# Half of one streamed weight chunk made resident, paid for with the output tail's second buffer and P_pad's own, with the tail's heads and stores moved to suit

## The chip, the cores and the metric

The kernel runs on one core of a Trainium2 chip. Times are device microseconds; lower is better. Every ratio compares fast runs of a kernel with fast runs of the kernel before on the same chip, one after the other. The experiments ran in five rounds on five chips: e1 to e4; e6 to e9 with e8; e10 to e13; e14 to e19; f29 and f3. Where two changed kernels of different rounds are compared below (e6 with e1, e13 with e6, e14 with e10), it is their ratios that are compared, and single profiled runs give the stage times. Ratios are the mean time of one kernel's fast runs over the mean time of the other's fast runs of the same rounds, so they are not quite the ratio of the medians quoted beside them. Brackets give the 95% interval of a ratio.

## The reference, cut to what matters

Two independent computations are joined along the last axis. The first (a long convolution) fills about the first 460 us and is not touched by the change. The second is a recurrent transformer: 64 segments of 32 new rows plus 8 memory rows go through a 32-head attention, and 8 rows of each result are the memory of the next segment.

```python
for s in range(n_seg):                       # 64 segments, strictly one after the other
    h = jnp.concatenate([mem, xs], axis=1)   # 8 memory rows + 32 rows of x
    q, k, v = (einsum('btd,dhe->bhte', h, W) for W in (Wq, Wk, Wv))
    scores = where(mask, einsum('bhqe,bhke->bhqk', q, k) * scale, -1e9)
    o = einsum('bhqk,bhke->bhqe', softmax(scores), v)
    o = einsum('bhte,hed->btd', o, Wo)
    mem = o[:, :M, :]                        # what the next segment waits for
    outs.append(o[:, M:, :])
```

## The kernel before: the parts that matter

The weights of the recurrent part are cut into 64 chunks of 128 partitions x 2048 bf16 (512 KB). In the order of use: 8 K, 8 Q (first half of the heads), 8 K, 8 Q (second half), 16 V, 16 output projection chunks. 43 stay in on-chip memory. 21 are "streamed"; two of these are kept in spare PSUM, so 19 are loaded from HBM in every segment, through a ring of six slots. A slot is refilled when PE has used its chunk:

```python
STREAM = (0, 1, 3, 7, 11, 15, 21, 23, 25, 29, 33, 36, 40, 43, 46, 49, 51, 53, 59, 60, 62)
KEPT = {18: "A", 6: "B"}          # positions in STREAM: chunks 59 and 21 are kept in PSUM
TURN = (6, 4)
INLINE = {1: 0, 3: 1, 5: 0, 11: 1, 12: 0, 14: 1}
...
def done(ch):                     # after the last matmul that reads chunk ch
    if ch in streamed:
        ...
        free.append(live.pop((now[0], ch))[0])
        ...
        if nxt in kept and s > 0: unkeep(s, kept[nxt])    # copy back from PSUM into the free slot
        else: fetch()                                     # start the next load
```

In each segment PE computes 32 of the 40 rows directly. The other eight, the last rows of each segment, are set aside in OTB and projected for two segments at once: the "output tail", 32 heads of four matmuls, one tail for a pair of segments. I call the first segment of a pair even, the second odd. The tail of a pair was run during the next pair: `TURN[0]` heads ahead of the hand-over of memory to the next segment, `TURN[1]` behind it, and the heads whose chunk is streamed while that chunk is in its slot ("inline"), three chunks in each segment. Its result goes out over the last rows of segments whose 32 rows (`Y`) were stored before.

```python
def store(self):
    YB = one.tile([128, 256], BF, tag="QT", name="YB")
    nc.vector.tensor_copy(YB[:], self.acc)
    for dq in range(4):
        nc.gpsimd.dma_start(...rows SEG*NB*b + NX ... of both segments..., YB[32 * dq:32 * dq + W, :])
...
hT, KBs, QBs = pend.pop(s)
VBs = one.tile([128, 2, 128], BF, tag="VBs", name="VBs")          # the V record, at the top of a segment
nc.gpsimd.dma_start(VBs[:]..., VBD[s]...)
...
Y = one.tile([128, 256], BF, tag="PT", name="Y")
nc.scalar.copy(Y[:], yacc[:, 0:256])
...
    tail.run(TURN[0])
    fill_mem(pend[s + 1][0], Y)                                   # the hand-over: rec <- tps <- Y
nc.gpsimd.dma_start(..., Y[:])
    tail.run(TURN[1])
```

A tile with a tag takes the memory of the last tile with that tag, and its first write waits until everything that used the old one has finished, DMA included. The instructions of each engine are issued in the order in which the program has them.

## Time and profile before

The median was 2196.6 us. The loop's hand-overs run from 459.4 us to 2156.6 us on the profile's scale.

| 700 to 2150 us | before |
|---|---|
| DMA share of 16 engines, rate | 1.01, 389 GB/s |
| PE busy | 1170 of 1450 us (81%) |
| DVE, ACT busy | 36%, 26% |
| granted TensorE clock | 0.99 |
| mean segment, even and odd (segments 10 to 59) | 26.46 and 26.99 us |

Windows view of the kernel before, the loop between 700 and 2150 us. Columns: the stretch and its length, then busy us and number of instructions of each engine, granted clock, DMA share, GB/s.

```profile
core 0: us, PE busy (x) PEld busy (x) DVE busy (x) ACT busy (x) POOL busy (x), PEclk, DMA share, GB/s
700.00:2150.00 1450.00, 1170.47 (x28793) 669.07 (x28781) 528.60 (x1904) 373.44 (x706) 257.38 (x811) 0.99 1.01 389
```

PE is idle a fifth of the time. The waits of PE in the same stretch (us in total, times, longest) say that it waits for streamed loads more than for anything else:

```profile
PE acc L873 <- DMA wring<-WS: 97.5, 218, 1.8
PE yacc L959 <- DMA wring<-WS: 47.7, 88, 1.6
PE SB L819 <- DVE SB L798: 28.8, 28, 1.2
PE SB L819 <- DVE SB L810: 17.7, 25, 0.7
```

The third line is tail heads that wait for the score masks to be written into the same PSUM bank, the fourth tail heads that wait for the tail's sums in that bank to be set to zero. Issues of DMA, from the page: size, and median us from issue to landing.

```profile
wring<-WS SPq DMA_DIRECT2D x1216, 512.0 KB, 7.4
VBs<-VBD POOLq DMA_DIRECT2D x64, 64.0 KB, 6.3
out_dram<-Y POOLq DMA_DIRECT2D x64, 64.0 KB, 6.3
out_dram<-YB POOLq DMA_DIRECT2D x128, 8.0 KB, 5.0
```

Each of these, even the one of 8 KB, has a median of 5 us or more to landing.

### The profile page before, as it was taken

The numbers are of one execution on the slowest core, as the hardware profiler recorded it, in microseconds if no ns is written. First come the engines' busy times: TensorE is split into PE (matmuls) and PEld (weight loads), VectorE is DVE, ScalarE is ACT, GpSimd is POOL, SyncE is SP. The second block draws the span as 40 slices with busy tenths as digits, with TensorE's granted clock in tenths as the row PEclk, the third lists the DMA queues.
The fourth block names the chain that finished last, engine by engine and source line by source line (L and its number), as shares of the span: only waits on it lengthen the run. The fifth ranks groups of instructions, "written<-read, shape, count | busy, mean of one in ns | idle before, by whom it ended". The sixth has DMA issues, their size and how long they took to land. (4 is left out here: it accounts for less than half of the span.)

```text
span 2195.6 us, 81532 instructions
## 1 busy us (share of the span) xinstructions
PE 1739.5 (79%) x35636; PEld 930.1 (42%) x35636; DVE 874.0 (40%) x2686; ACT 648.3 (30%) x1139; POOL 444.4 (20%) x1139
## 2 busy tenths in 40 slices
PE   4687886878778878788888887887878787888886
PEld 2232233334444444444444444444544444444444
DVE  8836752123333333333333333333333333333333
ACT  7845530122222222222222222222222222222222
POOL 5013432201112111111111111111112211111111
PEclk9888998999999999999999999999999999999999
DMA  9998869979999999999999999999999999999997
GB/s 336 338 346 297 279 230 331 336 262 395 373 380 388 382 383 391 389 386 384 390 392 395 392 394 390 392 396 386 390 383 386 389 383 383 392 392 383 386 389 270
DMA packets 261678, 804.66 MB, mean 366 GB/s; under 512 B 52332, under 2 KB 52364, under 8 KB 261319
## 3 DMA queue, kind: packets, MB, share of 16 engines
q1 hardware_dynamic: 227816, 721.58, 86.2%
q0 software_dynamic: 28272, 67.31, 9.2%
q10 hardware_dynamic: 5232, 10.55, 1.5%
q8 instruction: 279, 4.57, 0.9%
q14 instruction: 79, 0.65, 0.1%
HBM read 739.92 MB, written 62.39 MB: 365 GB/s over the span
## 5 line engine op out<-in xcount | busy, mean ns | idle before, releaser
L873 PEld LDWEIGHTS <-rec 128*32 128x32 bf16 x12351 | 322.4, 96 | 470.9 <-issue 252.0
L873 PE MATMUL acc<-wring,rec 128*32 128x512 bf16 (+1 forms) x3777 | 375.6, 385 | 137.0 <-DMA wring<-WS 123.7
L882 ACT CAST qkv_sb<-acc 128x512 bf16<-128x512 f32 x384 | 225.1, 586 | 657.1 <-PE acc L873 657.1
L959 PEld LDWEIGHTS <-OT 128*32 128x32 bf16 x8192 | 218.7, 97 | 181.0 <-issue 153.2
L959 PE MATMUL yacc<-wring,OT 128*32 128x256 bf16 x3072 | 154.7, 277 | 100.7 <-DMA wring<-WS 58.5
L873 PE MATMUL acc<-Wmid,rec 128*32 128x512 bf16 x3072 | 226.6, 385 | 0.0
L873 PE MATMUL acc<-Wres,rec 128*32 128x512 bf16 x2816 | 222.3, 382 | 0.0
L819 PEld LDWEIGHTS <-OTB 128*16 128x16 bf16 x4096 | 104.9, 90 | 102.8 <-issue 92.6
L945 ACT CAST OT<-OTp 128x512 bf16<-128x512 f32 x128 | 75.1, 586 | 242.1 <-PE OTp L937 242.1
L975 DVE COPY KT<-tps 128x512 bf16<-128x512 bf16 x64 | 27.2, 425 | 298.7 <-PE tps L888 298.7
L774 POOL DMA_DIRECT2D rec<-REC x64 | 37.5, 585 | 519.4 <-issue 282.7
L946 DVE CAST OTB<-OTp 128x128 bf16<-128x128 f32 x128 | 37.4, 292 | 260.4 <-ACT OT L945 260.4
L725 DVE TENSOR_SCALAR wring<-OTp 128x384 int32<-128x384 int32 x126 | 112.3, 891 | 59.3 <-PE acc L873 49.0
L873 PE MATMUL acc<-pw,rec 128*32 128x512 bf16 x1536 | 130.3, 382 | 0.0
L849 POOL COPY KT<-rec 128x128 bf16<-128x128 bf16 x128 | 38.8, 303 | 426.8 <-PE SB L897 422.7
L834 POOL DMA_DIRECT2D out_dram<-YB x128 | 73.3, 579 | 238.5 <-DVE YB L832 225.3
L903 DVE TENSOR_REDUCE mx<-SB 128x5 f32<-128x200 f32 x128 | 47.1, 368 | 175.8 <-PE SB L897 175.8
L819 PE MATMUL SB<-wring,OTB 128*16 128x256 bf16 x1488 | 78.8, 275 | 39.7 <-DVE SB L798 32.6
L888 PE MATMUL tps<-ident,qkv_sb 128*128 128x128 bf16 x1024 | 101.0, 221 | 8.2 <-DVE wring L725 0.2
L888 PEld LDWEIGHTS <-qkv_sb 128*128 128x128 bf16 x1024 | 62.7, 97 | 105.6 <-ACT qkv_sb L882 65.4
L1015 ACT CAST Y<-yacc 128x256 bf16<-128x256 f32 x64 | 23.8, 373 | 248.0 <-PE yacc L959 244.1
L959 PE MATMUL yacc<-Wlate,OT 128*32 128x256 bf16 x2048 | 94.4, 276 | 2.2 <-issue 2.1
(231 smaller groups left out, 2706.3 us busy)
## 6 DMA issues: line engine op xcount, KB each, us to landing
wring<-WS SPq DMA_DIRECT2D x1216, 512.0 KB, 7.4
rec<-REC POOLq DMA_DIRECT2D x64, 192.0 KB, 6.1
SK<-s_sb SPq DMA_DIRECT2D x16, 512.0 KB, 5.9
SU<-s_sb SPq DMA_DIRECT2D x16, 512.0 KB, 4.9
Kg<-SK ACTq DMA_DIRECT2D x32, 256.0 KB, 4.8
Ug<-SU SPq DMA_DIRECT2D x32, 256.0 KB, 5.3
REC<-stage POOLq DMA_DIRECT2D x16, 512.0 KB, 9.0
SZ<-zs SPq DMA_DIRECT2D x31, 256.0 KB, 5.2
```

What stands on the lines that cost most here:

```text
L725: nc.vector.tensor_scalar(out=dst, in0=src, scalar1=0, scalar2=None, op0=ALU.bitwise_or)
L774: nc.gpsimd.dma_start(rec[:], REC[:, s, :])
L819: nc.tensor.matmul(self.acc[32 * dq:32 * dq + W, x - o:y - o], lhsT=self.OTB[:, c, 4 * g + i, :], rhs=r, start=first and not self.seeded, ...
L834: nc.gpsimd.dma_start(bass.AP(outb.tensor, outb.offset + (SEG * NB * self.b + NX) * 2048 + 256 * dq, [[2048 * SEG, NB], [2048, 8], [1, 256 ...
L849: nc.gpsimd.tensor_copy(KT[:, :, :, 32:40], KBs[:, 128 * g:128 * g + 128].rearrange("p (c i t) -> p i c t", c=4, i=4))
L873: nc.tensor.matmul(self.acc[32 * c:32 * c + 32, x - 512 * c:y - 512 * c], lhsT=hT[:, kc, :], rhs=r, start=(kc == 0 and x == 512 * c), stop ...
L882: nc.scalar.copy(sb[:], self.acc[:])
L888: nc.tensor.transpose(tp[:, i * 128:(i + 1) * 128], sb[:, i * 128:(i + 1) * 128], ident[:])
L903: nc.vector.tensor_reduce(out=mx[:], in_=S, op=ALU.max, axis=AX.X)
L945: nc.scalar.copy(OT[:], o_view[:, :, :, 0:32])
L946: nc.vector.tensor_copy(OTB[:, :, 4 * g:4 * g + 4, 8 * j:8 * j + 8], o_view[:, :, :, 32:40])
L959: nc.tensor.matmul(yacc[32 * dq:32 * dq + 32, x - o:y - o], lhsT=OT[:, c, i, :], rhs=r, start=(h == 0 and x == o), stop=(h == 31), tile_po ...
```

## The change

The intent is to stream less: half of chunk 3 (a K chunk) becomes resident, 256 KB fewer per segment. That needs 2 KB per partition. By the tile sizes, a single OTB frees 1 KB, and P_pad, which now shares the slots of QT and KT, 640 B; the pool of the softmax's two small tiles also goes from two buffers to one, and they share one tag. The tail's result, which had shared QT's slot, is now stored from the slot of the V record. With one OTB, the tail of a pair has to be finished before the next pair writes OTB, so its heads move up: all inline heads into the odd segment, 4 and 6 at the odd-to-even turn, 10 in the next K projection. Core of the diff:

```diff
-TURN = (6, 4)
-INLINE = {1: 0, 3: 1, 5: 0, 11: 1, 12: 0, 14: 1}
+TURN = (4, 6)
+HALF = 3
...
+    half = order[HALF]
+    WH = ring.tile([128, 1024], BF, name="WH")
+    nc.gpsimd.dma_start(WH[:], dram_chunk(half)[:, 0:1024])
...                                          # fetch(): columns 1024 to 2048 only, for that chunk
-    two = ctx.enter_context(tc.tile_pool(name="b_two", bufs=2, side="right", reuse_waits="tile"))
+    two = ctx.enter_context(tc.tile_pool(name="b_two", bufs=1, side="right", reuse_waits="tile"))
...
-    P_pad = one.tile([128, 5, 64], BF, name="P_pad")
-    nc.vector.memset(P_pad[:], 0.0)
...
-                YB = one.tile([128, 256], BF, tag="QT", name="YB")
+                YB = one.tile([128, 256], BF, tag="VBs", name="YB")
...
-            VBs = one.tile([128, 2, 128], BF, tag="VBs", name="VBs")     # top of the segment
-            nc.gpsimd.dma_start(VBs[:]..., VBD[s]...)
...
-            def softmax_a():
+            def softmax_a(g):
+                P_pad = one.tile([128, 5, 64], BF, tag="KT" if g else "QT", name="P_pad")
+                nc.gpsimd.memset(P_pad[:, 0:4, 32:64], 0.0)
...                                          # softmax_b: seed_scores() taken out
-                        if last or INLINE[hp] == j:
+                    if j == NB - 1 and ch in streamed:
                             tail.head(2 * hp, w)
...
-            k0 = Proj(0, 0).run().evac()
+            k0 = Proj(0, 0)
+            for n in (3, 3, 32, 0):
+                k0.run(2)
+                more_tail(n)                 # in even segments; the last head triggers store()
+            k0 = k0.evac()
             q0 = Proj(1, 0).run(4)
             KT0 = keys(0)
             last_queries(0)
+            VBs = one.tile([128, 2, 128], BF, tag="VBs", name="VBs")
+            nc.gpsimd.dma_start(VBs[:]..., VBD[s]...)
...
+            if j == NB - 1:
+                tail = Tail(OTB, b)          # its zeroing, now in the middle of the odd segment
...
+            PT0 = softmax_b(P0)
+            seed_scores()                    # masks for the second half of the heads
...
-            if j == NB - 1 and not last:
-                tail = Tail(OTB, b)
...
                 fill_mem(pend[s + 1][0], Y)
+                seed_scores()                # masks for the next segment
```

More of the change, by code (lines that the diff above doesn't have):

```diff
@@ L644, in fetch @@
             live[s, ch] = k, t = slot()
-            (nc.gpsimd if k > 3 and s == 0 and len(live) < 3 else nc.sync).dma_start(t[:], stream_src(ch))
+            c = slice(1024 if ch == half else 0, 2048)
+            eng = nc.gpsimd if k > 3 and s == 0 and len(live) < 3 else nc.sync
+            eng.dma_start(t[:, c], stream_src(ch)[:, c])
     def place(ch, ap):
@@ L742, in pieces @@
         t = live[now[0], ch][1]
+        if ch == half:
+            return [(0, 1024, WH[:]), (1024, 2048, t[:, 1024:2048])]
         if kept.get(ch) == "B" and now[0] > 0:
@@ L803, in b_kernel, with __init__ @@
         class Tail:
-            def __init__(self, OTB, b, acc=None):
-                self.OTB, self.b, self.acc = OTB, b, tacc if acc is None else acc
-                self.seeded = acc is None
+            def __init__(self, OTB, b):
+                self.OTB, self.b, self.acc = OTB, b, tacc
                 self.left = list(range(32))
@@ L813, in head @@
                 g, c, i = h // 16, (h % 16) // 4, h % 4
-                first = len(self.left) == 32
                 self.left.remove(h)
@@ L820, in head @@
                                          lhsT=self.OTB[:, c, 4 * g + i, :], rhs=r,
-                                         start=first and not self.seeded, stop=not self.left,
+                                         start=False, stop=not self.left,
                                          skip_group_check=True, tile_position=(0, 32 * dq))
@@ L836, in store @@
                                 [[2048 * SEG, NB], [2048, 8], [1, 256]]), YB[32 * dq:32 * dq + W, :])
-        OTB = tail = own = None
+        OTB = tail = None
         for s in range(n_seg):
@@ L843, in b_kernel @@
             hT, KBs, QBs = pend.pop(s)
-            VBs = one.tile([128, 2, 128], BF, tag="VBs", name="VBs")
-            nc.gpsimd.dma_start(VBs[:].rearrange("p g e -> p (g e)"), VBD[s].rearrange("t c i w -> (c i) t w"))
             def keys(g):
@@ L906, in softmax_a, with softmax_b @@
                 nc.scalar.activation(S, S, ACT.Exp, scale=scale)
-            def softmax_b():
-                ssum = two.tile([128, 5], F32, tag="ssum", name="ssum")
+                return P_pad
+            def softmax_b(P_pad):
+                ssum = two.tile([128, 5], F32, tag="mx", name="ssum")
                 nc.vector.tensor_reduce(out=ssum[:], in_=S, op=ALU.add, axis=AX.X)
@@ L925, in softmax_b @@
                     nc.vector.transpose(out=PT[:, kb, :, 32:40], in_=P_pad[:, 4, ks])
-                seed_scores()
                 return PT
@@ L961, in out_proj, with more_tail @@
                                                  tile_position=(0, 32 * dq))
-                    if tail is not None and 2 * hp in tail.left and (ch in streamed or last):
-                        if last or INLINE[hp] == j:
-                            tail.head(2 * hp, w)
-                            tail.head(2 * hp + 1, w)
-                    if own is not None and ch in streamed:
-                        own.head(2 * hp, w)
-                        own.head(2 * hp + 1, w)
-                    done(ch)
-            k0 = Proj(0, 0).run().evac()
+                    if j == NB - 1 and ch in streamed:
+                        tail.head(2 * hp, w)
+                        tail.head(2 * hp + 1, w)
+                    done(ch)
+            def more_tail(n):
+                if tail is not None and j == 0:
+                    tail.run(n)
+            k0 = Proj(0, 0)
[3 more added lines that the diff above has]
+            k0 = k0.evac()
             q0 = Proj(1, 0).run(4)
@@ L974, in b_kernel @@
             last_queries(0)
+            VBs = one.tile([128, 2, 128], BF, tag="VBs", name="VBs")
+            nc.gpsimd.dma_start(VBs[:].rearrange("p g e -> p (g e)"), VBD[s].rearrange("t c i w -> (c i) t w"))
             nc.vector.tensor_copy(KT0[:, :, :, 0:32], transposes(k0))
@@ L981, in b_kernel @@
             scores(0, QT0, KT0)
-            softmax_a()
+            P0 = softmax_a(0)
+            if j == NB - 1:
+                tail = Tail(OTB, b)
             q1 = Proj(1, 1).run(4)
@@ L986, in b_kernel @@
             nc.scalar.copy(KT1[:, :, :, 0:32], transposes(k1))
-            PT0 = softmax_b()
+            PT0 = softmax_b(P0)
+            seed_scores()
             q1 = q1.run(4).evac()
@@ L993, in b_kernel @@
             scores(1, QT1, KT1)
-            softmax_a()
+            P1 = softmax_a(1)
             pv1 = Proj(2, 1).run(4)
             if j == 0:
-                OTB_new = one.tile([128, 4, 8, 8 * NB], BF, tag=f"OTB{b % 2}", name="OTB")
-                OTB = OTB_new
+                OTB = one.tile([128, 4, 8, 8 * NB], BF, tag="OTB", name="OTB")
             attend(0, PT0, V0)
             OT0 = evac_o(0)
-            PT1 = softmax_b()
+            PT1 = softmax_b(P1)
             pv1.run(4)
@@ L1006, in b_kernel @@
             yacc = ps_acc.tile([128, 512], F32, tag="acc", name="yacc")
-            if last:
-                own = Tail(OTB, b, ps_acc.tile([128, 512], F32, tag="acc", name="own_acc")[:, 0:256])
             out_proj(range(0, 5), OT0)
@@ L1015, in b_kernel @@
             nc.scalar.copy(Y[:], yacc[:, 0:256])
-            if j == NB - 1 and not last:
-                tail = Tail(OTB, b)
-            if tail is not None and not last:
+            if j == NB - 1:
                 tail.run(TURN[0])
@@ L1021, in b_kernel @@
                 fill_mem(pend[s + 1][0], Y)
+                seed_scores()
             nc.gpsimd.dma_start(bass.AP(outb.tensor, outb.offset + SEG * s * 2048, [[256, 4], [2048, 32], [1, 256]]), Y[:])
-            if tail is not None and not last:
-                tail.run(TURN[1])
-            if last:
-                own.run(32)
+            if j == NB - 1:
+                tail.run(32 if last else TURN[1])
 @with_exitstack
```

## The prediction

> **What bounds the kernel now.** After a prologue of about 470 us the kernel runs 64 recurrent segments. The times of the write that hands memory to the next segment (rec<-tps) lie 26.64 us apart on average over the loop. In the windows view, from 700 us on the DMA share is 1.01 to 1.02 at 387 to 391 GB/s, while PE is busy 80 to 81%, DVE 36%, ACT 26%. The DMA issues table shows what fills it: 1216 streamed loads wring<-WS of 512 KB, 19 per segment. The DMA records between 700 and 2100 us put 95.8% of the 16 engines' time on those loads (4096 B packets, mean 169 ns, median 162). The chain of waits is led by the same loads, and one-microsecond windows across two segments show the DMA share falling clearly below 0.9 only once. So the loop's period is the DMA engines' time. PE waits for it: about 97.5 us (K, Q, V projections) and 47.7 us (output projection) over 54 segments in the view of waits, 2.7 us a segment.
>
> **What the change does.**
> - Half of the third streamed K chunk becomes resident. Each segment moves 18.5 chunks instead of 19. A half chunk is 128 rows of 2048 B. In the prologue's DMA records such packets have median 84 ns beside 159 ns for 4096 B, so halving them nearly halves the time, without a small-packet penalty. The Trainium skill (DMA: Bandwidth & Descriptors, Specifications) puts the line-rate minimum at 512 B; the trace agrees. Estimate per segment: 128 x (169-88)/16 ns = 0.65 us; over 63 to 64 segments 41 us. One load of 256 KB is added to the prologue, which is mostly DMA-busy: about +0.7 us.
> - The tail's 32 heads (about 0.11 us of PE each, read from 16 matmuls in 0.6 us on the timeline) are only moved: 12 inline into the odd segment's output projection, 4 and 6 around the odd-to-even turn, 10 into the following K projection, where PE waits for DMA anyhow. The even-to-odd turn loses its 10. PE work is the same.
> - Seeding masks (0.5 us DVE) moves behind the memory hand-over; it ended 28.8 us of PE waits in the inline heads. That was PE slack, not DMA time: expected gain near zero.
> - P_pad is rewritten: two small POOL memsets a segment, off the chain.
> - The V record now waits for the output tail's stores to land (median 5.0 us) in even segments, then takes about 6.3 us itself. I estimate it lands 16 to 18 us into the segment, about when the first attention needs it (16 us): PE may stall 1 to 2 us there. With five loads (some 6.7 us) outstanding DMA should not starve, so I count at most 0.2 us a segment.
>
> **Sum.** 2196.5 - 41 + 0.7 = 2156 us, 1.8% less; just short of 2%. Range 2146 to 2171. Chances: faster by over 2% 0.25, within 2% 0.74, slower 0.01.
>
> **What would show it.** DMA share in the loop stays 1.01 or so; bytes fall by about 16.6 MB; period 26.0 us; WS loads 1152 of 512 KB and 64 of 256 KB; 2048 B packets near 88 ns. PE share rises to 82%, PE's DMA waits fall by at most 0.65 us a segment. Wrong if DMA share falls below 0.98 while PE waits for VBs or for DVE longer.
>
> **What would make it wrong.** The V record landing late enough to empty the DMA queue (less gain, 2165 to 2180); packets slowed around the hand-over (187 ns there against 163 ns elsewhere, when software-queue stores and loads run beside) becoming fewer or more; the new load delaying the prologue's gpsimd queue by several us; half-row reads costing more than 88 ns.

## The result, and the profile after

The change is slower: 2278.3 us median of 4 (2263.4 to 2289.9) against 2196.6, ratio 1.0365 [1.0301, 1.0428]. The profiled one is the fastest of them. The stream did shrink as intended (804.66 to 788.14 MB in all), but the loop's rate fell by more. The windows view after, columns as above:

```profile
700.00:2150.00 1450.00, 1149.58 (x27578) 662.67 (x27576) 507.37 (x1817) 353.03 (x673) 262.90 (x884) 0.95 0.97 363
```

DMA is no longer full (0.97), the granted clock is lower (0.95), and fewer instructions fit into the same 1450 us. The issues, as before:

```profile
wring<-WS SPq DMA_DIRECT2D x1152, 512.0 KB, 7.1
wring<-WS SPq DMA_DIRECT2D x64, 256.0 KB, 6.9
VBs<-VBD POOLq DMA_DIRECT2D x64, 64.0 KB, 6.0
out_dram<-YB POOLq DMA_DIRECT2D x128, 8.0 KB, 5.6
```

Waits in the loop (700 to 2150 us). The first five did not exist before; the last two are PE's waits for streamed loads, to be set beside the 97.5 and 47.7 us of before:

```profile
POOL VBs L983 <- DMA out_dram<-YB: 81.4, 18, 5.7
DVE P_pad L919 <- POOL P_pad L904: 61.6, 26, 3.5
POOL out_dram L837 <- DMA out_dram<-Y: 52.0, 9, 6.9
PE SB L895 <- ACT QT L1003: 44.3, 26, 2.5
PE OTp L940 <- DMA VBs<-VBD: 41.9, 26, 2.4
PE acc L874 <- DMA wring<-WS: 74.6, 131, 2.0
PE yacc L962 <- DMA wring<-WS: 20.6, 53, 1.3
```

PE's waits for streamed loads fell from 145.2 to 95.2 us. The bytes saved are not the reason: e2, which has the rest of the change and streams every chunk whole, shows nearly the same (its view of PE's waits, 700 to 2150 us):

```profile
PE acc L870 <- DMA wring<-WS: 81.7, 149, 2.2
PE yacc L958 <- DMA wring<-WS: 20.7, 57, 0.9
```

It fits that PE is late for other reasons and finds the loads there. Two new waits of PE, 44.3 and 41.9 us, happen 26 times each: once in every even segment. One even segment of the timeline (start us, length us, engine, line, what; in brackets the idle time before it and what ended it) shows where they come from. The memory hand-over is the copy at 1018.81.

```profile
1018.73 0.73 POOL L1030 DMA_DIRECT2D out_dram<-Y  x1 [6.96 <-ACT Y L1024]
1018.81 0.19 DVE L786 COPY rec<-tps 128x64 bf16<-128x64 bf16 x1 [2.91 <-PE tps L785]
1022.79 0.42 DVE L835 CAST YB<-SB 128x256 bf16<-128x256 f32 x1 [3.32 <-PE SB L822]
1025.85 2.25 POOL L837 DMA_DIRECT2D out_dram<-YB  x4 [6.39 <-DMA out_dram<-Y]
1028.09 0.30 POOL L850 COPY KT<-rec 128x128 bf16<-128x128 bf16 x1
1033.21 0.55 POOL L983 DMA_DIRECT2D VBs<-VBD  x1 [4.24 <-DMA out_dram<-YB]
1033.75 0.22 POOL L904 MEMSET P_pad<- 128x128 bf16 x1
1034.01 0.19 DVE L919 TENSOR_TENSOR P_pad<-SB,ssum 128x32 bf16<-128x32 f32 x1 [2.55 <-POOL P_pad L904]
1035.06 0.58 ACT L1003 COPY QT<-tps 128x512 bf16<-128x512 bf16 x1 [2.96 <-DVE PT L929]
1035.70 0.20 PE L895 MATMUL SB<-KT,QT 128*32 128x40 bf16 x4 [2.12 <-ACT QT L1003]
1038.52 0.22 PE L940 MATMUL OTp<-PT,VBs 32*128 32x40 bf16 x4 [0.54 <-DMA VBs<-VBD]
```

Read it from the top. The tail's result is ready at 1022.79, but its four stores start only at 1025.85, when Y's store has landed: both write the same last rows of the output, so the order is real. The load of the V record takes the slot from which the tail is stored, so it waits at 1033.21 for these stores to land. It sits in POOL's program order ahead of the memset of P_pad, so that memset waits too, then P, then QT (which takes P_pad's slot), then PE's second scores, idle for 2.12 us. The V record itself then lands later still: the first attention waits for it once more. Three DMA landings in a row, about 7, 5 and 5 us from issue (the second counted from the last of its four stores, which take 2.25 us to issue), fill the first 19 us of the segment.

The same, as means over the segments 10 to 59, worked out from the instruction records of the traces (us after the hand-over; e1 and e6 are mended versions explained below):

```
even segments                  before   after      e1      e6
tail's stores begin              0.40    5.88   22.90   22.58
V record's load issued           1.75   13.57    1.39    1.45
P_pad memset, first half            -   14.10    9.70    9.38
first transpose of P            10.78   14.63   12.09   11.76
first matmul that reads V       15.70   19.19   16.44   16.16
last output projection, end     25.08   27.05   25.60   25.26
length of the segment           26.46   27.85   26.48   26.12
odd segments
first matmul that reads V       15.70   16.69   16.44   16.37
last output projection, end     25.15   27.01   26.76   26.64
length of the segment           26.99   27.94   27.76   27.54
```

Even segments lose 3.5 us up to the V product and win 2.1 us back behind it, where the twelve tail heads of the kernel before are gone and PE's waits for the output projection's loads have shrunk. Odd segments lose 0.95 us, and the table says where: 1.0 us of it is there by the V product, while from V to the hand-over they take 11.25 us where they took 11.29 before. So the second loss is not at their end. The loads are behind by then: in odd segments the last packet of chunk 7 comes 1.6 to 1.7 us after the hand-over in the change, in e1 and in e6, and 0.8 us after it before (from the DMA records). These means are of one profiled run each; e11, a kernel whose time is level with before, shows 26.40 and 27.34 us for even and odd segments, so 0.3 us of such a difference need not mean anything.

### The profile page after: what moved, and what is told of

It is laid out like the page before. It is cut to its first block, busy times and chain, and to the rows that moved or that the text cites. A ratio compares the mean times of both kernels' runs of the same rounds, so it can differ in the third digit from the quotient of the medians.

```text
span 2260.8 us, 81857 instructions
## 1 busy us (share of the span) xinstructions
PE 1771.4 (78%) x35636; PEld 954.7 (42%) x35636; DVE 875.1 (39%) x2683; ACT 644.6 (29%) x1139; POOL 463.8 (21%) x1268
## 2 busy tenths in 40 slices
DMA packets 261759, 788.14 MB, mean 349 GB/s; under 512 B 52348, under 2 KB 52380, under 8 KB 261399
## 5 line engine op out<-in xcount | busy, mean ns | idle before, releaser
L874 PE MATMUL acc<-wring,rec 128*32 128x512 bf16 (+1 forms) x3649 | 386.3, 393 | 114.9 <-DMA wring<-WS 98.5
L962 PEld LDWEIGHTS <-OT 128*32 128x32 bf16 x8192 | 236.8, 104 | 158.9 <-issue 122.1
L874 PE MATMUL acc<-Wres,rec 128*32 128x512 bf16 x2816 | 238.6, 405 | 0.0
L874 PE MATMUL acc<-Wmid,rec 128*32 128x512 bf16 x3072 | 233.2, 393 | 0.0
L962 PE MATMUL yacc<-wring,OT 128*32 128x256 bf16 x3072 | 169.9, 299 | 67.0 <-DMA wring<-WS 28.0
L822 PEld LDWEIGHTS <-OTB 128*16 128x16 bf16 x4096 | 118.6, 91 | 77.9 <-issue 56.2
L1030 POOL DMA_DIRECT2D out_dram<-Y x64 | 46.6, 728 | 444.8 <-ACT Y L1024 438.1
L904 POOL MEMSET P_pad<- 128x128 bf16 x128 | 26.7, 209 | 455.6 <-PE SB L898 453.8
L962 PE MATMUL yacc<-Wlate,OT 128*32 128x256 bf16 x2048 | 106.2, 307 | 1.3 <-issue 1.3
L962 PE MATMUL yacc<-Wmore,OT 128*32 128x256 bf16 x2048 | 89.5, 290 | 7.7 <-issue 7.3
```

Source lines behind the costliest of these rows:

```text
L822: nc.tensor.matmul(self.acc[32 * dq:32 * dq + W, x - o:y - o], lhsT=self.OTB[:, c, 4 * g + i, :], rhs=r, start=False, stop=not self.left, ...
L874: nc.tensor.matmul(self.acc[32 * c:32 * c + 32, x - 512 * c:y - 512 * c], lhsT=hT[:, kc, :], rhs=r, start=(kc == 0 and x == 512 * c), stop ...
L962: nc.tensor.matmul(yacc[32 * dq:32 * dq + 32, x - o:y - o], lhsT=OT[:, c, i, :], rhs=r, start=(h == 0 and x == o), stop=(h == 31), tile_po ...
L1030: nc.gpsimd.dma_start(bass.AP(outb.tensor, outb.offset + SEG * s * 2048, [[256, 4], [2048, 32], [1, 256]]), Y[:])
```

## The experiments

Eighteen more kernels ran. All were correct unless said otherwise. "e" and "f" names are labels.

| label | what | median us | ratio to before |
|---|---|---|---|
| after | the change | 2278.3 | 1.0365 [1.0301, 1.0428] |
| e1 | tail stored late | 2219.9 | 1.0115 [1.0080, 1.0149] |
| e2 | change without the half chunk | 2295.7 | 1.0451 [1.0411, 1.0491] |
| e3 | V load behind POOL's other work | 2286.5 | 1.0418 [1.0372, 1.0465] |
| e4 | idle PE kept busy | 2267.7 | 1.0342 [1.0297, 1.0387] |
| e6 | e1, seeds last | 2201.3 | 1.0066 [1.0027, 1.0105] |
| e7 | e1, seeds as before the change | 2209.0 | 1.0069 [1.0046, 1.0092] |
| e9 | e1, no tail heads behind the hand-over | 2206.6 | 1.0063 [1.0046, 1.0080] |
| e13 | e6 without the half chunk | 2219.9 | 1.0123 [1.0092, 1.0155] |
| e19 | e6 less six tail heads (wrong result) | 2175.2 | 0.9926 [0.9889, 0.9963] |
| e10 | before, half of chunk 3 not loaded | 2198.0 | 1.0026 [0.9997, 1.0055] |
| e14 | before, half of chunk 29 not loaded | 2167.6 | 0.9891 [0.9864, 0.9919] |
| e12 | before, 3/4 of every load (wrong result) | 2041.9 | 0.9329 [0.9290, 0.9367] |
| e11 | before, P_pad shared | 2195.9 | 1.0021 [0.9989, 1.0053] |
| e8 | e11, 384 columns of chunk 3 resident | 2200.0 | 1.0029 [1.0004, 1.0053] |
| e17 | e11, 384 columns of chunk 29 resident | 2189.1 | 0.9998 [0.9964, 1.0032] |
| e16 | e6, half of chunk 29 instead of 3 | 2206.4 | 1.0076 [1.0038, 1.0115] |
| f29, f3 (5 runs) | tail spread again, half of 29 or of 3 | 2217.2, 2240.5 | 1.0108 [1.0074, 1.0142], 1.0209 [1.0188, 1.0230] |

### The V record's chain: e1, e2, e3, e4

e1 moves the store of the tail to where nothing depends on it, and leaves the shared slot, the V load and everything else alone.

```diff
-                if not self.left:
-                    self.store()
...
             OT1 = evac_o(1)
+            if tail is not None and j == 0:
+                tail.store()
```

> Edit: the changed kernel, but the tail's result is copied out of PSUM and stored only after the second attention of the even segment (about 21 us in) instead of in its K projection (about 4 us in). By then the V slot is free until the next segment and both Y stores have landed, so neither the tail store nor the V load has anything to wait for that matters. Theory A (the V record's load waits for the tail store to land, which waits for the Y store to land; the POOL queue stands behind that wait): V issue in even segments falls from 13.6 us to about 1.6 us, PE no longer idles ahead of the second scores, the DMA share returns to 1.01, granted clock back to about 0.97, time 2150 to 2170. Theory B (the half chunk, its 2 KB reads or the emptier ring, costs the time): little change, over 2230. Theory C (the tail heads gathered into the odd segment's output projection overload PE): over 2220, odd segments stay near 27.9 us.

Measured: 1.0115. V is issued at 1.39 us instead of 13.57, PE's wait for QT in even segments is gone, even segments are back to 26.48 us. Of PE's waits in the loop, those for VBs no longer appear. This is 2.5 points of the 3.65 lost (about 55 us), so the chain is the largest cause. But the 2150 to 2170 that theory A promised was missed by 50 us: odd segments stayed at 27.76, as theory C had it; whether for its reason is taken up at e19. The DMA share in the loop came back to 0.99 only:

```profile
700.00:2150.00 1450.00, 1173.92 (x28347) 676.05 (x28340) 518.53 (x1876) 367.29 (x696) 270.28 (x905) 0.97 0.99 373
```

e2 takes the half chunk back and keeps the rest of the change.

```diff
-            c = slice(1024 if ch == half else 0, 2048)
+            c = slice(0, 2048)
```

> Edit: the changed kernel with the half chunk taken back: all 19 chunks are streamed whole, everything else as changed. Theory A: the stall is untouched and bounds the loop, so the half chunk was worth little here: 2265 to 2310. Theory B: back to about 2197. Theory C: 2265 to 2310, like A.

Measured: 1.0451, slower than the change. So the half chunk does no harm by itself (theory B falls) and may be worth about 0.9 of a point, some 19 us, inside the stalled schedule; the two intervals overlap. (The change and e2 ran in different rounds; their ratios are each to the kernel before beside them.)

e3 moves the V load behind the second key and query copies on POOL, so that POOL's queue no longer blocks.

```diff
             KT1 = keys(1)
             last_queries(1)
+            VBs = one.tile(...); nc.gpsimd.dma_start(VBs..., VBD[s]...)
```

> Edit: the changed kernel with the V load issued behind the second key and query copies on the POOL queue, so that P_pad's memset and those copies no longer stand behind its wait, while the V record still lands late. Theory A splits here: if the queue's blocking is the larger part, the first P_pad memset returns to about 10 us, PT0 to about 12 us, PE idles for V alone (landing still near 19 us) and the time falls to 2210 to 2250; if the late landing is the larger part, 2255 or more. Theories B and C: no change, 2263 to 2290.

Measured: 1.0418. The P_pad memset is back at 9.74 us and the first transpose of P at 12.14, so the queue was unblocked as intended, yet the V product starts at 19.85 us and PE's wait for VBs doubled:

```profile
PE OTp L940 <- DMA VBs<-VBD: 88.0, 31, 6.2
```

The blocked queue and the late landing are parallel consequences of one chain. e3 shows that the late landing alone is long enough to cost all that the change lost: with the queue free, the wait moves to the V record (which landed at 19.8 us in e3 and at 19.1 in the change). What the blocked queue would cost alone was not run.

e4 asks about the clock. In the change, the halved clock (0.5 for about 3.4 us at a time, in the clock records) struck in 28 of 31 even segments, mostly 17 to 22 us in, after PE had been busy for 28 to 61% of the five microseconds before. e4 repeats four transposes eight times in the idle stretch.

```diff
+            for _ in range(8 if j == 0 else 0):
+                transposes(q1)
             nc.scalar.copy(QT1[:], transposes(q1))
```

> Edit: the changed kernel with eight more rounds of the same four 128-column transposes of q1 in even segments, ahead of the wait for QT1 (32 more matmuls, some 1.8 us of PE in an idle stretch of about 2 us; results unchanged). If the halved clock after that idle stretch (28 of 31 even segments) is a consequence of the idle and itself costs time: halved-clock time in the loop falls from 171 us to under 60 us and the time falls by 20 to 50 us, to 2220 to 2255. If the halved clock is harmless or has another cause: same as the changed kernel (2263 to 2290) or slower by the added work.

Measured: the halved time in the loop (from the second segment on) fell from 171 to 85 us, but the ratio is 1.0342 beside 1.0365, well within the intervals. The windows view of e4, to be set beside the change's (clock 0.95, DMA share 0.97):

```profile
700.00:2150.00 1450.00, 1170.61 (x28455) 696.38 (x28448) 509.35 (x1822) 356.14 (x677) 263.31 (x886) 0.98 0.98 363
```

Removing half of the halved time bought nothing that can be told from noise. So the lower clock looks like a sign of the stall more than a cause of the loss; its other half was not removed.

### The turn: e6, e7, e9

In the change, the masks are seeded on DVE right behind the hand-over, and the six tail heads that follow use the same PSUM bank, so PE waits for the seeds. Timeline of e1 at one such turn:

```profile
1066.67 0.19 DVE L786 COPY rec<-tps 128x64 bf16<-128x64 bf16 x1 [4.54 <-PE tps L785]
1067.13 0.20 DVE L803 CAST SB<-mask 128x40 f32<-128x40 bf16 x1
1067.39 1.46 PE L822 MATMUL SB<-Wlate,OTB 128*16 128x256 bf16 x24 [0.76 <-DVE SB L803]
1068.62 1.08 PE L873 MATMUL acc<-wring,rec 128*32 128x512 bf16 x8
```

The K projection, which everything waits for, starts 1.95 us after the hand-over (with the clock halved just then; the mean over even segments 10 to 59 is 1.47 us, and 1.48 in the change). In the kernel before it started 0.28 us after at the turn shown, and 0.38 in the mean:

```profile
1701.10 0.19 DVE L781 COPY rec<-tps 128x64 bf16<-128x64 bf16 x1 [1.19 <-issue]
1701.38 0.60 PE L873 MATMUL acc<-wring,rec 128*32 128x512 bf16 x8
```

Three edits of e1 remove this wait in different ways: e6 seeds after the six heads; e7 seeds in the softmax as before the change; e9 leaves no heads there (`TURN = (4, 0)`, and 5, 5 and the rest in the K projection).

```diff
                 fill_mem(pend[s + 1][0], Y)
-                seed_scores()
...
                 tail.run(32 if last else TURN[1])
+                seed_scores()                       # e6
```

> Edit: e1 (tail stored late), and the masks are seeded after the six tail heads that follow the memory hand-over instead of ahead of them. In e1 those heads wait for the seeds (PE idle 0.76 us before them in one odd-to-even turn, 20 us in 26 waits), and the K projection starts 1.95 us after the hand-over copy where it took 0.3 us before the change. Theory D (what is left of the loss is the turn: seeds ahead of heads ahead of the K projection, while the ring is full and DMA idles, share 0.68 in the first microsecond of even segments): K starts about 1 us earlier in even segments, time 2190 to 2208. Theory C (the twelve heads inside the odd output projection are what is left): little change, 2213 to 2225.

> Edit: e1 with the seeding undone: the masks are written right behind the transposes of P, as in the kernel before. Theory D: the turn loses the wait for seeds, but the first inline heads of the odd segment wait for them again (about 1 us, as before the change): 2190 to 2212. Theory C: 2213 to 2225.

> Edit: e1 with no tail heads between the memory hand-over and the K projection: 4 before the hand-over as now, none after it, then 5, 5 and the rest after two, four and six K chunks (seeds stay where the change put them, and nothing at the turn waits for them). Theory D: K starts within 0.5 us of the hand-over copy in even segments, DMA share at the turn back over 0.9, time 2180 to 2205, at or below e6. Theory C: 2213 to 2225.

Measured: 1.0066, 1.0069 and 1.0063. Three ways to the same result, about half a point (11 us) below e1's 1.0115. The traces show the wait going: the K projection starts 0.78, 0.67 and 0.25 us after the hand-over in even segments (means), where it took 1.47 in e1. That this is worth half a point is less sure. The intervals of e6 and e1 overlap; the three agree, but they share one round and its runs of the kernel before, and e1 ran on another chip. e9 starts K earliest and gains no more than the others. (The expectation's DMA share of 0.68 at the turn is that of single turns; the mean over e1's even segments is 0.94.) e7's seeds behind the softmax cost as little as e6's: moving the seeds gained nothing in either place, and what harm it did was ahead of the heads.

### The heads at the end of the odd segment: e19

e19 leaves out the tail heads of head pairs 11, 12 and 14 in the odd output projection (wrong result).

```diff
                     if j == NB - 1 and ch in streamed:
-                        tail.head(2 * hp, w)
-                        tail.head(2 * hp + 1, w)
+                        if hp < 11:
+                            tail.head(2 * hp, w)
+                            tail.head(2 * hp + 1, w)
+                        else:
+                            tail.left = [h for h in tail.left if h // 2 != hp]
```

> Edit (wrong result on purpose): e6 without the six tail heads of head pairs 11, 12 and 14 in the odd output projection (0.11 us each, 0.64 us of PE a pair of segments). Theory C (heads gathered at the end of the odd output projection lie on PE's own chain and lengthen it): the odd segment falls by about 0.6 us, the time by 15 to 25 us, 2176 to 2186. If PE had slack there: within 6 us of e6.

Measured: 0.9926 against e6's 1.0066, about 30 us. In the profiled runs the odd segment fell from 27.54 to 26.59 us and the even one rose from 26.12 to 26.38, which makes about 21 us. Six heads take about 0.64 us of PE, 20 us over 31 pairs: at least all of it showed up as time, in a kernel whose PE is idle a fifth of the time. The heads at the end of the odd output projection stand between the second attention and the hand-over, with no slack. (e19 does less work in all, so it is a measure of the place, not a fix.) It does not show that moving the heads there lengthened the odd segment against the kernel before. Four of the six, those of pairs 11 and 14, ran there before too; ahead of the odd hand-over there were 12 heads before and 16 after, but before they also waited for the zeroing of the tail's sums (the 17.7 us in the first view of waits), and this wait is gone. From V to the hand-over the odd segment takes as long as before, as the table above shows.

### The saved bytes: e10 to e14, e8, e11, e17

The forecast's main term was 0.65 us of DMA time a segment. e10 takes exactly that saving in the kernel before, without paying for memory: half of chunk 3 is not loaded, and its columns are read from another resident chunk. The sums are wrong, though the comparison's tolerance passed it.

```diff
+            c = slice(1024 if ch == order[3] else 0, 2048)
...
+        if ch == order[3]:
+            return [(0, 1024, res[order[2]][:, 0:1024]), (1024, 2048, t[:, 1024:2048])]
```

> Edit (wrong result on purpose): the kernel before, in which the third streamed chunk's load brings only its second half, and the K projection reads the first half from another resident chunk of the same shape. It is the change's saving of 256 KB a segment alone, without its memory and without its schedule. If streamed bytes set the loop's time, as the prediction had it: 0.65 us a segment, 2197 - 41 = 2150 to 2162. If the kernel before is held as much by PE's own chain, so that the saved DMA time reappears as idle DMA around the turn: 2175 to 2200.

Measured: 1.0026 [0.9997, 1.0055]. The saving is worth nothing that can be told from noise, where 41 us were forecast. (In the profiled run even segments are 0.15 us shorter than before's and odd ones 0.54 us longer; the second was not followed up.) The windows view (700 to 2100 us) of before, then of e10, shows what became of it: the rate fell with the bytes.

```profile
700.00:2100.00 1400.00, 1130.08 (x27835) 645.61 (x27820) 510.59 (x1836) 360.27 (x681) 247.87 (x781) 0.99 1.01 389
```

```profile
700.00:2100.00 1400.00, 1122.42 (x27623) 640.41 (x27621) 505.77 (x1820) 357.37 (x677) 246.30 (x780) 0.99 0.99 376
```

e12 asks whether bytes matter at all: three quarters of every streamed load but the kept chunks'.

```diff
+            c = slice(512 if ch not in kept else 0, 2048)
```

> Edit (wrong result on purpose): the kernel before, with every streamed load but the two kept chunks' cut to 1536 of 2048 columns (the rest read from a resident chunk). DMA needs some 20 us a segment. The time then shows PE's own chain with the DMA far from full. If bytes were the sole limit: about 6 us a segment less until PE stops it; PE is busy 21.5 us of 26.6, so a floor of 23 to 24 us, 1960 to 2030. If PE's chain is as long as the DMA's: floor of 25.5 or more, 2120 or more.

Measured: 0.9329, 2042 us, a mean segment of 24.35 us against 26.80. Just above the range for a limit by bytes alone, and far below the other one; the DMA share was 0.94. So bytes do matter, but not chunk 3's.

A likely reason can be read off the times of the loads. I attributed the DMA records to loads in their order, and took means over segments 12 to 60 of the kernel before (even ones; us from the hand-over of the segment that uses the chunk):

```
chunk   issued  last packet        chunk   issued  last packet
  0      -9.9      -3.8              15     -2.0       3.8
  1      -8.6      -2.4              23      0.9       5.1
  3      -7.1      -0.9              29      1.9       8.1
  7      -3.5       0.4              ...
 11      -3.0       1.8              62     15.7      21.3
```

Chunk 3 is the last load before a pause: between 7.1 and 3.5 us ahead of the hand-over PE frees no slot for a load, because it is in the second attention and in resident chunks (and one slot goes to a kept chunk). Then chunk 7 is issued. In that stretch PE's own chain sets the pace. A shorter chunk 3 lets DMA finish sooner, and then it has nothing to do until chunk 7 is issued. In e10 the first packet of chunk 7 comes 1.7 us after its issue, in the kernel before 2.3. e14 is e10 with one number changed: chunk 29 (Q), loaded while PE waits for loads. (The expectations call it the eighth streamed chunk; counted without the kept ones it is the ninth. Its sums are wrong too.)

```diff
-            c = slice(1024 if ch == order[3] else 0, 2048)
+            c = slice(1024 if ch == order[29] else 0, 2048)
```

> Edit (wrong sums on purpose): as e10, the kernel before with half of one chunk's load skipped, but the eighth streamed chunk (query, second half of heads) instead of the third. Shadow theory (only bytes loaded while PE waits for loads count): 0.4 to 0.65 us a segment, 2152 to 2172 or 1.2 to 1.9% faster. Rival (PE's chain is the limit everywhere, or a byte is worth nothing because the ring, not the bytes, sets the pace): as e10, within 0.4% of before.

Measured: 0.9891, 1.35 points below e10. That is 0.37 us a segment (23 us over 63), a little under the lower end of what was expected. The windows view of e14, where the rate is also lower but the DMA share is back at 1.01:

```profile
700.00:2100.00 1400.00, 1134.22 (x28153) 650.45 (x28148) 516.42 (x1856) 363.96 (x689) 251.18 (x792) 0.99 1.01 383
```

The DMA share of the six microseconds around the even-to-odd hand-over (24 to 30 us after the even one), means over 21 pairs (segments 12 to 53) from the DMA records, shows where most of e10's saving went: into idle DMA, some 0.45 us at this hand-over; the other one shows much the same.

```
before   1.01 0.99 1.00 1.01 0.98 0.97
e10      0.88 0.90 0.93 0.90 0.93 0.95
e14      1.01 1.00 0.99 0.99 1.01 1.00
```

e11, e8 and e17 are correct kernels: before with P_pad in shared slots (e11), and with the 384 columns that then fit, of chunk 3 (e8) or of chunk 29 (e17).

```diff
+HALF = 3            # e17: 29
+WHC = 384
+                P_pad = one.tile([128, 5, 64], BF, tag="KT" if g else "QT", name="P_pad")
+                nc.gpsimd.memset(P_pad[:, 0:4, 32:64], 0.0)
```

> Edit: the kernel before with P_pad in the slots of QT and KT and its memsets on POOL, nothing resident. It splits e8 (384 columns resident with shared P_pad, 0.3% slower). If the shared slots cost what the 384 columns saved: 2208 to 2220. If the shared slots are free and bytes are worth nothing here: 2193 to 2203.

> Edit: the kernel before, with 384 of the 2048 columns of the same K chunk resident (what fits once P_pad shares the slots of QT and KT, as in the change); tail, V load and seeds as before. If streamed bytes set the loop's time in the kernel before: 384/2048 of 1.35 us, 0.25 us a segment, 16 us in all: 2176 to 2186, ratio about 0.993. If the resident part is worth nothing or shared P_pad costs: 2195 or more.

> Edit: e8 with the 384 resident columns taken from the eighth streamed chunk instead of the third; a correct kernel with the tail, V load and seeds of before. Shadow theory: 0.15 to 0.25 us a segment below before, 10 to 16 us, 2176 to 2186. Rival: as e8, 2193 to 2203.

Measured: 1.0021, 1.0029 and 0.9998. Shared P_pad is nearly free. e8's saving of 16 us did not come, as that reason would have it. e17 is below e8 in the expected direction, but its 10 to 16 us did not come either; the intervals overlap, so I don't count it as support.

### The saving in the mended schedule, and an attempt to beat both: e13, e16, f29, f3

e13 is e6 with all chunks streamed whole (the same edit as e2); e16 is e6 with `HALF = 29`.

> Edit: e6 (tail stored late, seeds last) with the half chunk taken back, all 19 chunks streamed whole. It tells what the half chunk is worth in the mended schedule, against e6 at 2201. If a byte saved is a time saved: 2236 to 2245. If not: 2201 to 2220.

> Edit: e6 with the resident half taken from the eighth streamed chunk instead of the third; a correct kernel. Shadow theory: faster than e6 (2201) by 10 to 30 us, 2170 to 2191. Rival: 2196 to 2206.

Measured: e13 1.0123 against e6's 1.0066, so chunk 3's half may be worth about 0.6 of a point (12 us) there, a third of what was forecast; the intervals overlap. And e13 shows the mended schedule's own cost: 1.2% (27 us) over before, with the same bytes. Its even segments take 26.12 us, no longer than before's 26.46, and its odd ones 28.23 against 26.99. e16 is a miss: 1.0076, no better than e6. Its odd segments were longer (28.09 us) and the halved clock was granted more often in its profiled run (140 us of the loop, against 72 in e6). Why chunk 29 did not pay there is open.

f29 and f3 spread the tail over both segments again: pairs 1, 3 and 5 inline in the odd segment, 11, 12 and 14 in the even one, the second half of OTB overwritten only after that, and the tail stored from QT's slot as in the kernel before.

```diff
-                    if j == NB - 1 and ch in streamed:
+                    if tail is not None and ch in streamed and (last or (j == 0) == (hp >= 8)):
...
             out_proj(range(0, 5), OT0)
+            if tail is not None and j == 0:
+                tail.run(10)
             attend(1, PT1, V1)
```

> A correct kernel meant to beat both: the change with the eighth streamed chunk halved, seeds last, and the tail spread again over both segments: in the odd segment only head pairs 1, 3 and 5 inline, 4 heads ahead of the hand-over, 3 and 3 in the next K projection; in the even segment the ten resident heads of the second half ahead of the second attention (where PE waits anyway) and pairs 11, 12 and 14 inline; OTB stays single because its second half is overwritten only after those. The tail result goes to the slot of QT as before the change, so the V load waits for nothing. With theories A, C and the shadow theory: 2155 to 2185. If the shared slots or the single OTB cost in another way: 2190 or more.

> Edit: f29 with the third streamed chunk halved instead of the eighth, as in the change. Shadow theory: slower than f29 by 10 to 35 us. Rival (which chunk is halved does not matter): within 5 us of f29.

Measured: 1.0108 and 1.0209. Neither beats the kernel before. Odd segments fell to 26.03 us in f29, below before's 26.99, but even ones rose to 28.12: the last output projection matmul came at 27.19 us instead of 25.08. From V to the hand-over even segments take 12.42 us instead of 10.76, with 16 tail heads in that stretch instead of 12; the heads are the likely cause, but the copy of OTB's second half was moved there too. A second new wait is in the view of waits of f29: QT's slot is not free until the tail's stores land.

```profile
DVE QT L993 <- DMA out_dram<-YB: 26.3, 15, 2.9
```

The pair does answer the question about bytes: f29 and f3 differ only in the chunk that is halved, and differ by a full point, about 23 us, in the direction e10 and e14 gave, with intervals far apart and on the same chip. No version that I ran with a correct result is faster than the kernel before beyond its interval (e17 is level); e14, whose sums are wrong, puts about 23 us on half of chunk 29 if 2 KB for it could be found without moving the tail; the correct e16 and e17 did not show their share of it.

## Why the prediction was wrong, point by point

Two steps of the prediction failed: that every saved microsecond of DMA time is a microsecond of the loop, and that the V record's wait costs almost nothing.

- **"So the loop's period is the DMA engines' time."** This step failed. A DMA share of 1.01 averaged over the loop did not mean that every byte counts. e10 removed the same bytes in the kernel before and gained nothing. The 0.65 us a segment was right as DMA time (2048 B packets measured 86 ns against 173 for 4096 B after the change, near the 88 and 169 estimated), but as a term of the sum it measured 0 in the kernel before, and perhaps 12 to 19 us in all in the change's own schedules (e13 to e6, e2 to after; intervals overlap), not 41. Chunk 29's half was worth 23 in e14. As the load times, e10 and e14 have it, the period is a loop of alternating limits: DMA from about chunk 7 into the value projections, PE's chain from the second attention to the hand-over.
- **"at most 0.2 us a segment" for the V record.** This step failed by more in size than any other: e1 prices it at 2.5 points, some 55 us, 0.9 us a segment. The mechanism was named, but its start was wrong. I counted two landings (tail store and V load) from the tail's end and had V at 16 to 18 us; the tail's stores themselves wait for Y's store to land first (they start at 5.9 us, though their data are ready at 4.3), and the four of them take 2.25 us to issue, so the V record landed at 19.1 and was used at 19.2. I also did not see that POOL runs in order, so the P_pad memset and the second key copy stood behind that wait; "two small POOL memsets a segment, off the chain" was wrong. And "With five loads (some 6.7 us) outstanding DMA should not starve" was wrong: PE fell behind and freed no slots, and the DMA share fell to 0.97. The prediction did name this sign (a share below 0.98 while PE waits for VBs) and this danger, but priced it as less gain, 2165 to 2180 us.
- **"[The heads] are only moved ... PE work is the same."** True as a sum, but the place has a price: six heads at the end of the odd segment cost at least their 0.64 us (e19: 21 to 30 us in all). Whether the move itself lengthened that stretch is not shown; from V to the hand-over it takes as long as before.
- **"Seeding ... expected gain near zero."** Right about gain; but its new place held up the tail heads and, by 1.1 us in the mean, the K projection: perhaps 11 us (e1 to e6, e7, e9).
- **Right:** the bytes and counts (1152 and 64 loads, 16.5 MB fewer), the packet times (2048 B packets took half the time of 4096 B ones, in keeping with the 512 B minimum that the prediction cites; no run went near 512 B), shared P_pad costing next to nothing by itself (e11). Right by another cause: PE's waits for DMA falling (e2 shows the same fall without the saving). Wrong: the 26.0 us period (27.9), a steady DMA share, PE at 82%. The mean of 26.64 us quoted for the kernel before was itself a little low; over all segments from the second on it is 26.80.
- The parts add up roughly: the schedule without the saving costs 99 us (e2), of which the chain is 55, the turn perhaps 11, and 27 are left in e13; the saving takes some 19 off. What is not settled: why e16 gained nothing from chunk 29, and the cause of the 27 us, which lie in the odd segments and mostly ahead of the V product (16.69 us in e13 against 15.70). Late loads, the clock and the shared slots were not told apart there.

## What to carry to other kernels

A resource that is busy all the time on average is the limit only where something waits for it: before pricing a saved transfer, find when that transfer is issued and whether anyone is waiting when it lands, and if a spare experiment is at hand, drop the transfer alone and look. When a buffer is shared between a store and a later load, add up every landing in the chain, from the store that must come first to the load that must come last, and check what else stands in the issuing engine's program order behind that wait. Work moved into an engine that is idle on average can be free only in a stretch where that engine waits; between the last dependence and the hand-over to the next step it cost at least its full length here (e19). And when a stage is slower, find by time marks in which half of it the loss arises before blaming what was moved there.

## What the Trainium skill lacked or had wrong

- **"DMA: Bandwidth & Descriptors", Anatomy of one DMA:** gives a fixed cost of about 2.0 us plus bytes, mostly the wait for the last byte to be confirmed. That fits the direction, not the size, when all engines are full: the 8 KB stores of the tail took 4.8, 5.6 and 7.0 us (minimum, median, maximum) from issue to landing here, and three dependent landings took up the first 19 us of a segment. The page's table of latencies has a figure at high load for an access to memory (2 us); I find none for a DMA that lands behind full queues.
- **"TensorE: Matmul & The Clock Gate", HAM oscillation:** states the rule as no idle gap over about 3.4 us. In the change the clock halved in 28 of 31 even segments, though PE's longest single wait in the loop was 2.5 us; PE had been busy for 28 to 61% of the five microseconds before. The page's next section does tell of one kernel whose clock swings from frequent short idles, but gives no busy share at which that happens. The halved intervals are 3.4 us long, or twice that, which is the length of the page's window.
- **None of the pages that I used** says that a full DMA share over a loop can hide loads without effect on its time (the nearest, "Perfetto Trace Analysis", Optimization Strategy, says that the most contended engine can change over time): 256 KB a segment off one load gave +0.3% (e10), off another -1.1% (e14).
